# Raw inputs in four loads with tiles of their own, and the output's decays through a DRAM scratch

## The chip, the cores and the metric

The kernel runs on one core of a Trainium2 chip. The metric is the device time of one execution in microseconds (us). Three runs of the kernel before took 1276.74, 1278.87 and 1279.15 us; their median, 1278.87, is the time before.

## What is computed

A recurrent attention runs over 768 positions for 4 x 8 batches and heads, each with a 40 x 40 state. Its output becomes the 3072 x 320 input of two dense layers in a row, each with 2048 hidden units.

```python
for t in range(S):                                        # r,k,v,w,a,b: (4, 8, 768, 40)
    y[:, :, t] = np.einsum('bhd,bhde->bhe', rt, state)
    Sa = np.einsum('bhde,bhe->bhd', state, at)
    state = state * wt[:, :, None, :] - np.einsum('bhd,bhe->bhde', Sa, bt) \
            + np.einsum('bhd,bhe->bhde', vt, kt)
x = y.transpose(0, 2, 1, 3).reshape(B * S, H * D)         # (3072, 320)
h = x @ w_in;   x = (h / (1 + exp(-h))) @ w_out           # first layer
h = x @ w2_in;  out = (h - tanh(h)) @ w2_out              # second layer
```

## The kernel before

The sequence is cut into 12 chunks of 64 positions, and a chunk into two halves of 16 heads (`hf` 0 and 1). In the first phase (to about 930 us) the attention of the chunks and the first layer run interleaved; in the second phase only the second layer runs. Weights are converted from float32 pairs on the way (lines 515 to 557: DMA into `cr`, then work on ACT, DVE and POOL; the second layer's go to a DRAM scratch `w2d`).

Within a chunk, each half goes through these steps.

- `load_raw` (L196) loads everything that the half's preparation needs in one DMA of 120 partitions x 2311 floats into the tile `raw`: 384 columns of a, 768 of k and b, 384 of r, 384 of v, 391 of w. `raw` has one buffer, so the load waits until the preparation before has read its last column (the POOL subtraction of L241). For half 1 of chunk 0, a free slot of the ring `LR` serves instead.
- `prep` (L210) makes the scaled operands. DVE scans w into `pq` (L226: the running product of the decays, restarted for each head), takes a reciprocal into `d1b` (L227), writes two columns of decays to `HL` (L228, L229), multiplies a by `pq` (L231), scans w backward into the same tile `pq` (L232: the inverse decays), and multiplies k and b by them (L235). ACT and POOL split the products into a high and a low float16 part in the tile `HL`, which has one buffer. Twelve DMAs (L252) then copy `HL` into a slot of the five-slot ring `LR`, three partition blocks of 40 each. A slot of the ring comes free when PE has used a half of an earlier chunk (its last readers are `ch_y` and `ch_x`).
- p1, sol, mrg, x, u, s, y and m are the attention proper: PE matmuls with evictions on ACT and DVE. `sol_step` is a forward substitution of 31 pairs of DVE instructions (L311, L313). The lows of u and of the state are copied across partitions by SP DMAs (`LR<-LR`, `LR<-lows` at L390; `MT` at L447 and L448; `M` at L477 and L478).
- `pf_load` (L480) loads the decays once more, in the layout of the transposed output (feature by position), from an input `wf` that the host packs: 128 x 384 floats into the one-buffered tile `pf`. `pf_scan` (L485) scans them on DVE (L487). `x_t1` transposes the output y on PE, and `x_t2` multiplies it by `pf` on DVE (L504) and splits it into xh and xl (ACT L505, POOL at the helper line L191), which also frees `pf`.

The order in which the instructions are written comes from a table of times (`SC`) and from dependencies (`when`); a scheduler then sets each engine's own order, and each engine runs its list strictly in that order. All DMAs stand in one list, that of SP. Each DMA takes one of eight counters in turn, and a DMA waits for the one that used its counter before. A DMA that waits holds up all behind it.

Of the kernel before, what the change touches and what calls it, by code (L numbers as in the profile page):

```python
# [13 lines left out]
ALU = mybir.AluOpType  # L14
# [33 lines left out]
def _poly():  # L48
# [46 lines left out]
    ps=(2.4285, 5.4475),  # L95
# [10 lines left out]
def build(tc, pk, tv, wf, w1i, w1o, w2i, w2o, out, nch=NCH, dbg=None):  # L106
# [41 lines left out]
    d1f = const.tile([128, 6, C], F16, name="d1f")  # L148
    POOL.memset(d1f, 0.0)
    POOL.memset(d1f[:, :, 0:1], P_INIT * S_X / (S_R * S_M))  # L150
# [37 lines left out]
    y_t, ps_t, x_t, pf_t = {}, {}, {}, {}  # L188

# [20 lines left out]
    def prep(c, hf):  # L210
        raw = raw_t.pop((c, hf))
# [20 lines left out]
        DVE.tensor_tensor_scan(pt[:, 2:391][:, ::-1], w[:, 2:391][:, ::-1], d1b[:, 2:391][:, ::-1], 0.0, ALU.mult, ALU.add)  # L232
        pi = pt[:, 2:392].rearrange("p (j t) -> p j t", t=65)[:, :, 0:C]
# [4 lines left out]
        pscale(raw[:, 1152:1920], raw[:, 1152:1920], S_R)  # L238
# [57 lines left out]
    def lr_slot():  # L296
        return at_p.tile([128, 16, RW], F16, tag="LR", name="LR", bufs=5)
# [198 lines left out]
    def x_t2(c, hf):  # L496
# [7 lines left out]
        DVE.tensor_tensor(xf, ps, xf, ALU.mult)  # L504
# [150 lines left out]
    for c in range(nch):  # L655
# [83 lines left out]
def pack(inputs, nch=NCH):  # L739
# [7 lines left out]
    def zero_first(x):  # L747
        return np.concatenate([np.zeros_like(x[..., :1]), x], axis=-1)
# [6 lines left out]
    wv = np.asarray(inputs["w"]).reshape(B, H, NCH, C, D).transpose(2, 1, 4, 0, 3).reshape(NCH, DM, B, C)  # L755
    wv = zero_first(wv[..., :-1]).reshape(NCH, DM, B * C)
    wf = np.stack([wv[:, 0:128], wv[:, 128:256], np.concatenate([wv[:, 256:320]] * 2, axis=1)], axis=2)
    wf = wf.reshape(NCH, 128, 3, 2, 128).transpose(0, 3, 1, 2, 4)

# [5 lines left out]
    def w_out(m):  # L765
# [3 lines left out]
        "pk": pk[:nch], "tv": tv[:nch], "wf": wf[:nch],  # L769
# [20 lines left out]
```

## Time and profile before

| | |
|---|---|
| median of three runs | 1278.87 us |
| profiled execution, device time | 1283.47 us |
| its span (first to last instruction) | 1281.4 us |
| PE, DVE, ACT, POOL busy in the span | 1063.9, 971.2, 822.5, 421.6 us |
| mean granted TensorE clock, share of full speed | 0.932 |
| DMAs moved | 122.36 MB in 154955 packets |

The profile is one execution, so its times add up to 1281.4 us of span and 2.1 us around it. The share of busy time is a mean over three stages: a prologue of about 160 us, in which PE has little to do; the stage from 160 to 885 us, in which attention and first layer run together; and the rest, in which PE is nearly full. A DVE or PE instruction that is late holds up everything behind it on its engine, so a wait matters where the engine is the one that others wait for.

### The profile page before, as it was taken

To read this page: it belongs to the slowest core of one execution; us is meant where nothing else is said; L and a number is where in the kernel's file an instruction comes from. 1 tells how busy PE (TensorE), PEld (TensorE's weight loads), DVE (VectorE), ACT (ScalarE), POOL (GpSimd) and SP (SyncE) were. 2 spreads that over 40 slices of the span, in tenths; PEclk is the share of its full clock that TensorE was granted. 3 is DMA by queue.
4 is the path that set the end of the run, shared out by engine and by line. 5 is a ranking of instruction groups with operands and counts; after the bars stand their busy time and mean duration, and the time that the engine had idled before them with its cause. 6 is when DMAs were issued, how large, how long until landed. Compare 5 with 4: busy or idle time off the path is not lost.

```text
span 1281.4 us, 31698 instructions
## 1 busy us (share of the span) xinstructions
PE 1063.9 (83%) x12624; PEld 879.2 (69%) x12624; DVE 971.2 (76%) x1871; ACT 822.5 (64%) x1586; POOL 421.6 (33%) x490
## 2 busy tenths in 40 slices
PE   0006578798889889889888998999999999999997
PEld 0005566677677667767776777888778888888885
DVE  6678998788887868878677787853238788888885
ACT  2456687666767657645545454554259888888886
POOL 5334544434424333423232231010013333333332
PEclk9999759879898979989897998999989999999999
DMA  5565665555656554353424432110701111111100
GB/s 129 144 146 154 173 155 138 146 146 147 159 143 171 141 160 114 101 116 96 108 74 96 108 94 74 31 47 21 216 24 24 24 33 27 33 25 24 24 12 21
DMA packets 154955, 122.36 MB, mean 95 GB/s; under 512 B 89528, under 2 KB 140152, under 8 KB 151928
## 3 DMA queue, kind: packets, MB, share of 16 engines
q1 hardware_dynamic: 154808, 120.35, 36.5%
q8 instruction: 99, 1.62, 0.5%
q14 instruction: 48, 0.39, 0.1%
HBM read 63.59 MB, written 13.89 MB: 60 GB/s over the span
## 4 chain that ended last, share of the span: by engine, by line
PE 22%; issue 18%; DMA 17%; DVE 17%; POOL 9%; SPq 8%; ACT 8%; POOLq 0%; DVEq 0%; ACTq 0%
DMA raw<-pk 8%; POOL gl L191 7%; PE hp L567 7%; SPq L252 5%; DMA LR<-HL 3%; DVE Tl L313 3%; DVE tmp L311 2%; PE o L589 2%; PE o L591 2%; PE o L590 2%; DMA pf<-wf 2%; SPq L632 2%; PE psx L361 2%; PE psu L376 1%; ACT cr L525 1%
## 5 line engine op out<-in xcount | busy, mean ns | idle before, releaser
L567 PE MATMUL hp<-xh,wih 128*128 128x256 f16 x960 | 196.7, 291 | 13.9 <-DVE gl L577 13.7
L567 PE MATMUL hp<-x,w 128*128 128x256 f16 x1344 | 189.5, 273 | 0.0
L191 POOL TENSOR_TENSOR gl<-q,gh 128x512 f16<-128x512 f32 x96 | 111.3, 1159 | 207.8 <-ACT gh L624 207.8
L567 PEld LDWEIGHTS <-wih 128*128 128x128 f16 x1344 | 131.9, 103 | 39.5 <-issue 15.4
L567 PEld LDWEIGHTS <-w 128*128 128x128 f16 x1344 | 131.5, 98 | 22.9
L313 DVE TENSOR_TENSOR Tl<-Tl,tmp 128x126 f32<-128x126 f32 (+22 forms) x372 | 130.3, 350 | 7.6
L311 DVE TENSOR_TENSOR tmp<-Al,Tl 128x126 f32<-128x126 f32 (+22 forms) x372 | 120.4, 324 | 8.2 <-ACT Al L303 1.2
L267 PE MATMUL p1a<-LR 120*128 120x64 f16 x384 | 28.5, 207 | 116.7 <-DMA LR<-HL 69.9
L589 PE MATMUL o<-woh,gh 128*128 128x320 f16 x384 | 120.0, 313 | 5.9 <-DVE x2o L600 5.3
L591 PE MATMUL o<-woh,gl 128*128 128x320 f16 x384 | 118.6, 315 | 2.7 <-DVE gl L577 2.7
L590 PE MATMUL o<-woh,gh 128*128 128x320 f16 x384 | 119.7, 312 | 0.0
L590 PE MATMUL o<-w,gh 128*128 128x320 f16 x384 | 112.5, 299 | 0.0
L589 PE MATMUL o<-w,gh 128*128 128x320 f16 x384 | 111.3, 299 | 1.4 <-ACT gh L624 1.3
L567 PE MATMUL hp<-xl,wih 128*128 128x256 f16 x384 | 111.6, 291 | 0.1
L267 PEld LDWEIGHTS <-LR 120*128 120x128 f16 x384 | 21.6, 105 | 123.5 <-issue 108.9
L591 PE MATMUL o<-w,gl 128*128 128x320 f16 x384 | 102.5, 299 | 1.0 <-POOL gl L191 1.0
L590 PEld LDWEIGHTS <-gh 128*128 128x128 f16 x768 | 76.7, 100 | 32.6 <-issue 5.5
L591 PEld LDWEIGHTS <-gl 128*128 128x128 f16 x768 | 76.4, 100 | 31.0 <-DVE gl L577 3.4
L589 PEld LDWEIGHTS <-gh 128*128 128x128 f16 x768 | 76.6, 100 | 30.0 <-ACT gh L624 2.0
L577 DVE SCALAR_TENSOR_TENSOR gl<-hp,gh 128x512 f16<-128x512 f32 x96 | 65.5, 682 | 41.2 <-ACT gh L576 37.8
L619 DVE SCALAR_TENSOR_TENSOR s<-s,z 128x512 f32<-128x512 f32 x96 | 70.7, 737 | 32.9 <-ACT s L617 31.8
L575 ACT ACTIVATE hp<-hp 128x512 f32<-128x512 f32 x96 | 56.2, 587 | 49.0 <-PE hp L568 47.0
(147 smaller groups left out, 2952.1 us busy)
## 6 DMA issues: line engine op xcount, KB each, us to landing
raw<-pk SPq DMA_DIRECT2D x23, 1083.3 KB
LR<-HL SPq DMA_DIRECT2D x92, 150.9 KB
cr<-w1i SPq DMA_DIRECT2D x16, 384.0 KB
cr<-w2i SPq DMA_DIRECT2D x16, 384.0 KB
cr<-w1o SPq DMA_DIRECT2D x16, 320.0 KB
cr<-w2o SPq DMA_DIRECT2D x16, 320.0 KB
w2d<-w2s SPq DMA_DIRECT2D x32, 160.0 KB
w<-w2d SPq DMA_DIRECT2D x4, 1280.0 KB
```

Source lines behind the costliest of these rows:

```text
L191: POOL.tensor_tensor(out, a, b, ALU.subtract)
L252: SP.dma_start(out=dst[pl * 40:pl * 40 + 40, :, d0:d0 + w], in_=src[:, :, s0:s0 + w])
L267: PE.matmul(pa[:, p, :], kb, R[:, u, p, 0:C], start=True, stop=True)
L311: DVE.tensor_tensor(tv_, Al[:, j + 1:, j:j + 1].to_broadcast([128, n, w]), Tl[:, j:j + 1, :w].to_broadcast([128, n, w]), ALU.mult)
L313: DVE.tensor_tensor(Tl[:, j + 1:, :w], Tl[:, j + 1:, :w], tv_, ALU.add)
L567: PE.matmul(o, wi[:, f, a], x[:, k], start=n == 0, stop=False)
L575: ACT.activation(out=hp, in_=hp, func=AF.Silu, scale=1.0 / (S_X * S_WI))
L577: DVE.scalar_tensor_tensor(out=gl, in0=hp, scalar=S_G, in1=gh, op0=ALU.mult, op1=ALU.subtract)
L589: PE.matmul(o, gh[:, cs], wo[:, f, 0], start=f == 0, stop=False)
L590: PE.matmul(o, gh[:, cs], wo[:, f, 1], start=False, stop=False)
L591: PE.matmul(o, gl[:, cs], wo[:, f, 0], start=False, stop=f == NF - 1)
L619: DVE.scalar_tensor_tensor(out=s, in0=s, scalar=GAMMA, in1=z, op0=ALU.add, op1=ALU.mult)
```

## The change

Two things are changed.

First, the raw inputs come in four DMAs, each into a tile of its own: w (391 columns, two buffers), a (384, two buffers), k and b together (768, one buffer), r and v together (768, one buffer). The backward scan no longer overwrites `pq`; it writes a tile `pr`.

Second, the host no longer packs `wf`. After the copies of `HL`, `prep` writes the forward scan (`pq`) to a DRAM scratch `pd`, feature by position, in four DMAs of 40 partitions with runs of 64 floats. `pf_load` reads its tile from there in three DMAs (one of 128 partitions with two runs of 128 floats each, two of 64 partitions). `pf_scan` is gone, with its constant `d1f`; the scale that stood in the constant moves into the multiplication of `x_t2`, which becomes a scalar_tensor_tensor.

```diff
     def load_raw(c, hf):
-        if c == 0 and hf == 1:
-            t = lr_slot().rearrange("p u n -> p (u n)").bitcast(F32)[0:120, 0:RAWN]
-        else:
-            t = at_p.tile([120, RAWN], F32, tag="raw", name="raw", bufs=1)
-        SP.dma_start(out=t, in_=pk[c, hf])
-        raw_t[c, hf] = t
+        spare = lr_slot().rearrange("p u n -> p (u n)").bitcast(F32)[0:120] if c == 0 and hf == 1 else None
+        raw_t[c, hf] = []
+        for nm, o, n, k in (("w", 1920, 391, 2), ("a", 0, 384, 2), ("kb", 384, 768, 1), ("rv", 1152, 768, 1)):
+            t = spare[:, o:o + n] if spare is not None else at_p.tile([120, n], F32, tag="raw" + nm, name="raw" + nm, bufs=k)
+            SP.dma_start(out=t, in_=pk[c, hf, :, o:o + n])
+            raw_t[c, hf].append(t)
...
         pt = at_p.tile([120, 392], F32, tag="pq", name="pq", bufs=1)
+        pr = at_p.tile([120, 392], F32, tag="pr", name="pr", bufs=1)
...
-        DVE.tensor_tensor_scan(pt[:, 2:391][:, ::-1], w[:, 2:391][:, ::-1], d1b[:, 2:391][:, ::-1], 0.0, ALU.mult, ALU.add)
-        pi = pt[:, 2:392].rearrange("p (j t) -> p j t", t=65)[:, :, 0:C]
+        DVE.tensor_tensor_scan(pr[:, 2:391][:, ::-1], w[:, 2:391][:, ::-1], d1b[:, 2:391][:, ::-1], 0.0, ALU.mult, ALU.add)
+        pi = pr[:, 2:392].rearrange("p (j t) -> p j t", t=65)[:, :, 0:C]
...
+        for i, j0, n, u in ((0, 0, 6, 0), (1, 0, 2, 0), (1, 2, 4, 1), (2, 0, 4, 1)):
+            h = 6 * i + j0 - 8 * u
+            SP.dma_start(out=pd[c, hf, 40 * h:40 * (h + n), u].rearrange("(h d) t -> d h t", d=40),
+                         in_=pq[40 * i:40 * i + 40, j0:j0 + n, 0:C])
...
     def pf_load(c, hf):
         t = at_p.tile([128, 3, 128], F32, tag="pf", name="pf", bufs=1)
-        SP.dma_start(out=t, in_=wf[c, hf])
+        v = pd[c, hf].rearrange("f u t -> f (u t)")
+        SP.dma_start(out=t[:, 0:2], in_=v[0:256].rearrange("(k p) n -> p k n", k=2))
+        for q in range(2):
+            SP.dma_start(out=t[64 * q:64 * q + 64, 2], in_=v[256:320])
         pf_t[c, hf] = t
-
-    def pf_scan(c, hf):
-        t = pf_t[c, hf].rearrange("p k n -> p (k n)")
-        DVE.tensor_tensor_scan(t, t, d1f.rearrange("p b t -> p (b t)"), 0.0, ALU.mult, ALU.add)
...
-        DVE.tensor_tensor(xf, ps, xf, ALU.mult)
+        DVE.scalar_tensor_tensor(out=xf, in0=ps, scalar=S_X * S_KB / (S_R * S_M), in1=xf, op0=ALU.mult, op1=ALU.mult)
```

The scheduler's order moves with it, at three places that the prediction speaks of. Line numbers of the changed kernel differ by a few from those before.

DVE at the start, the first preparation and the beginning of the second. Before:

```order
L226 SCALAR_TENSOR_TENSOR pq<-raw,d1a 120x390
L227 RECIPROCAL d1b<-pq 120x6
L228 TENSOR_SCALAR HL<-pq 120x6
L231 SCALAR_TENSOR_TENSOR raw<-raw,pq 120x384
L229 SCALAR_TENSOR_TENSOR HL<-pq,HL 120x6
L487 SCALAR_TENSOR_TENSOR pf<-pf,d1f 128x384
L232 SCALAR_TENSOR_TENSOR pq<-raw,d1b 120x389
L235 TENSOR_TENSOR raw<-raw,pq 120x768
L226 SCALAR_TENSOR_TENSOR pq<-LR,d1a 120x390
```

After:

```order
L222 SCALAR_TENSOR_TENSOR pq<-raww,d1a 120x390
L223 RECIPROCAL d1b<-pq 120x6
L224 TENSOR_SCALAR HL<-pq 120x6
L227 SCALAR_TENSOR_TENSOR rawa<-rawa,pq 120x384
L228 SCALAR_TENSOR_TENSOR pr<-raww,d1b 120x389
L225 SCALAR_TENSOR_TENSOR HL<-pq,HL 120x6
L231 TENSOR_TENSOR rawkb<-rawkb,pr 120x768
L222 SCALAR_TENSOR_TENSOR pq<-LR,d1a 120x390
```

The scan of `pf` between the two scans of w is gone, and the backward scan (now L228) no longer stands behind the second column of `HL`.

DVE in the middle of the kernel, at the end of a chunk's substitution (`Tl`), where the second half's preparation writes `HL`. Before:

```order
L437 SCALAR_TENSOR_TENSOR Md<-psm,p_2155 40x320 [waits PE_49,Pool_49]
L323 STREAM_TRANSPOSE W_143<-Al 32x32x32 [waits Activation_49]
L324 STREAM_TRANSPOSE TT_119<-Al 64x32x32
L504 TENSOR_TENSOR pf<-psyt,pf 128x384 [waits PE_49]
L275 TENSOR_TENSOR mK_122<-p1a,mask_k 64x512 [waits PE_49]
L228 TENSOR_SCALAR HL<-pq 120x6 [waits DMAHW4_49,DMAHW7_49,DMAHW2_49,DMAHW0_49]
L437 SCALAR_TENSOR_TENSOR Md<-psm,p_2155 40x320 [waits Pool_49]
L229 SCALAR_TENSOR_TENSOR HL<-pq,HL 120x6 [waits DVE_49]
L232 SCALAR_TENSOR_TENSOR pq<-raw,d1b 120x389 [waits DVE_49]
L235 TENSOR_TENSOR raw<-raw,pq 120x768 [waits DVE_49]
```

After:

```order
L224 TENSOR_SCALAR HL<-pq 120x6 [waits DMAHW5_49,DMAHW6_49,DMAHW2_49,DMAHW0_49]
L504 SCALAR_TENSOR_TENSOR pf<-psyt,pf 128x384 [waits PE_49]
L225 SCALAR_TENSOR_TENSOR HL<-pq,HL 120x6 [waits DVE_49]
L438 SCALAR_TENSOR_TENSOR Md<-psm,p_2242 40x320 [waits Pool_49]
L276 TENSOR_TENSOR mK_119<-p1a,mask_k 64x512 [waits PE_49]
L324 STREAM_TRANSPOSE W_140<-Al 32x32x32 [waits Activation_49]
L325 STREAM_TRANSPOSE TT_116<-Al 64x32x32
L222 SCALAR_TENSOR_TENSOR pq<-raww,d1a 120x390 [waits DVE_49]
L223 RECIPROCAL d1b<-pq 120x6 [waits DVE_49]
L227 SCALAR_TENSOR_TENSOR rawa<-rawa,pq 120x384
L228 SCALAR_TENSOR_TENSOR pr<-raww,d1b 120x389 [waits DVE_49]
```

Once `HL` is free, only two short writes are left for the second half; its backward scan and its k and b product stand some 60 instructions earlier, and the rows behind are already the scans of the next chunk's first half.

SP in the middle of the kernel, from the last copies of `HL` of a half to the next raw loads. Before:

```order
L482 DMA pf<-wf 128x384
L252 DMA LR<-HL 40x4x322
L201 DMA raw<-pk 120x2311
L602 DMA x2d<-x2o 128x2x384
L557 DMA w2d<-w2s 128x640
L515 DMA cr<-w2i 128x768
L477 DMA M<-M 40x640
L478 DMA M<-lows 40x640
```

After:

```order
L199 DMA rawkb<-pk 120x768
L199 DMA rawrv<-pk 120x768
L484 DMA pf<-pd 128x2x128
L486 DMA pf<-pd 64x128 x2
L478 DMA M<-M 40x640
L479 DMA M<-lows 40x640
L256 DMA pd<-pq 40x6x64
L256 DMA pd<-pq 40x2x64
L256 DMA pd<-pq 40x4x64
L478 DMA M<-M 40x640
L479 DMA M<-lows 40x640
L256 DMA pd<-pq 40x4x64
```

Where one raw load and one load of `pf` stood, there are two raw loads (the two others stand earlier), three loads of `pf` and the four writes of `pd`, the last two of them between and behind the copies of M.

## Rows read from the trace of the kernel before

**Rows 1.** Busy time by stretch: start:end, length, PE, PEld, DVE, ACT, POOL, granted clock, DMA.

```profile
160.00:885.00 725.00, 636.38 (x8816) 529.89 (x8817) 565.75 (x1222) 442.12 (x885) 234.28 (x281) 0.90 0.44 114
400.00:480.00 80.00, 69.66 (x901) 56.74 (x901) 62.07 (x135) 49.03 (x100) 27.48 (x34) 0.85 0.59 157
320.00:400.00 80.00, 68.86 (x953) 55.99 (x951) 67.61 (x143) 60.65 (x119) 33.33 (x41) 0.91 0.56 153
800.00:880.00 80.00, 79.45 (x1215) 67.58 (x1211) 46.95 (x108) 41.01 (x84) 7.25 (x10) 0.98 0.14 36
930.00:1281.00 351.00, 342.90 (x2811) 275.42 (x2810) 272.66 (x392) 283.95 (x517) 112.59 (x99) 0.99 0.10 24
```

**Rows 2.** Chain that ended last, 160 to 885 us (first row) and pieces: start, us, what.

```profile
by line: DMA raw<-pk 13.2%; PE hp L567 7.4%; SPq L252 6.6%; issue 5.5%; DMA LR<-HL 3.7%; DVE Tl L313 3.1%; PE psx L361 2.9%; PE psu L376 2.6%; DVE tmp L311 2.4%; PE o L589 2.0%; PE o L591 1.9%; PE o L590 1.9%; PE psy L420 1.8%; PE mg L345 1
491.49 1.55 POOL HL L241
493.06 7.46 DMA raw<-pk
...
525.07 2.60 DMA LR<-HL
```

**Rows 3.** Waits, 160 to 885 us: engine, line, waited for, us, times, longest.

```profile
DVE pq L226 <- DMA raw<-pk: 40.5, 16, 4.6
DVE pf L487 <- DMA pf<-wf: 19.3, 10, 2.9
...
SPq L482 <- POOL xl L191: 23.7, 11, 6.8
...
SPq L390 <- ACT LR L386: 16.0, 6, 5.6
SPq L252 <- PE psm L429: 15.4, 5, 6.2
```

**Rows 4.** Groups of DVE instructions, 160 to 885 us: busy us, mean ns, idle before.

```profile
L487 DVE TENSOR_TENSOR_SCAN pf<-pf,d1f 128x384 f32<-128x384 f32 x22 | 22.9, 1042 | 19.4 <-DMA pf<-wf 19.3
L232 DVE TENSOR_TENSOR_SCAN pq<-raw,d1b 120x389 f32<-120x389 f32 x18 | 21.4, 1187 | 0.2
L235 DVE TENSOR_TENSOR raw<-raw,pq 120x768 f32<-120x768 f32 x18 | 20.3, 1130 | 0.2
L226 DVE TENSOR_TENSOR_SCAN pq<-raw,d1a 120x390 f32<-120x390 f32 x18 | 17.7, 981 | 40.6 <-DMA raw<-pk 40.5
```

**Rows 5.** DVE in one chunk: start, us, line, instruction, idle before it.

```profile
500.54 0.97 DVE L226 TENSOR_TENSOR_SCAN pq<-raw,d1a 120x390 f32<-120x390 f32 x1 [1.02 <-DMA raw<-pk]
...
527.79 0.18 DVE L228 TENSOR_SCALAR HL<-pq 120x6 f16<-120x6 f32 x1 [0.98 <-DMA LR<-HL]
...
534.19 0.94 DVE L235 TENSOR_TENSOR raw<-raw,pq 120x768 f32<-120x768 f32 x1
```

**Rows 6.** The prologue: start, us, engine, line, instruction, idle before it.

```profile
9.31 0.97 DVE L226 TENSOR_TENSOR_SCAN pq<-raw,d1a 120x390 f32<-120x390 f32 x1 [1.71 <-DMA raw<-pk]
...
15.65 3.81 POOL L191 TENSOR_TENSOR HL<-raw,HL 120x384 f16<-120x384 f32 x3
15.89 1.43 DVE L487 TENSOR_TENSOR_SCAN pf<-pf,d1f 128x384 f32<-128x384 f32 x1 [4.42 <-DMA pf<-wf]
17.25 1.56 DVE L232 TENSOR_TENSOR_SCAN pq<-raw,d1b 120x389 f32<-120x389 f32 x1
...
21.86 1.62 DVE L241 TENSOR_TENSOR HL<-raw,HL 120x768 f16<-120x768 f32 x1
```

**Rows 7.** DMA issues on SP: durations min/median/max in ns, and one issue of 64 partitions.

```profile
L252 SPq DMA_DIRECT2D LR<-HL x276: 767/772/1358, 12.3 to 791.1; - x138
...
L201 SPq DMA_DIRECT2D raw<-pk x23: 351/509/585, 0.8 to 750.6; - x23
...
L482 SPq DMA_DIRECT2D pf<-wf x24: 332/368/466, 1.7 to 896.6; - x24
...
515.65 0.54 SPq L207 DMA_DIRECT2D VU<-tv  x1
```

**Rows 8.** DMA packets, 160 to 885 us: queue, packets, MB, share of 16 engines.

```profile
q1 hardware_dynamic: 103966, 81.33, 43.6%
```

More of the change, by code (lines that the diff above doesn't have):

```diff
@@ L94 @@
     pl=(-0.631, 4.8433),
-    ps=(2.4285, 5.4475),
     xt=(5.6773, 6.5083),
@@ L103, with build @@
 )
-def build(tc, pk, tv, wf, w1i, w1o, w2i, w2o, out, nch=NCH, dbg=None):
+def build(tc, pk, tv, w1i, w1o, w2i, w2o, out, nch=NCH, dbg=None):
     nc = tc.nc
@@ L147, in build @@
         msk[nm] = m
-    d1f = const.tile([128, 6, C], F16, name="d1f")
-    POOL.memset(d1f, 0.0)
-    POOL.memset(d1f[:, :, 0:1], P_INIT * S_X / (S_R * S_M))
     gam = const.tile([128, 1], F32, name="gam")
@@ L188, in build @@
     y_t, ps_t, x_t, pf_t = {}, {}, {}, {}
+    pd = dram.tile([nch, 2, DM, 2, C], F32, name="pd")
     def psub(out, a, b):
@@ L210, in prep @@
     def prep(c, hf):
-        raw = raw_t.pop((c, hf))
+        w, ra, rkb, rrv = raw_t.pop((c, hf))
         hl = HL
@@ L217, in prep @@
         k0, v0 = (0, 2 * C) if c % 2 == 0 else (C, 0)
-        def sl(i, n):
-            return raw[:, i:i + 6 * n].rearrange("p (j t) -> p j t", t=n)
-        av, kb, rv, vv, w = sl(0, C), sl(384, 2 * C), sl(1152, C), sl(1536, C), raw[:, 1920:RAWN]
+        av, kb, rv, vv = [x.rearrange("p (j t) -> p j t", j=6) for x in (ra, rkb, rrv[:, 0:384], rrv[:, 384:768])]
         pt = at_p.tile([120, 392], F32, tag="pq", name="pq", bufs=1)
+        pr = at_p.tile([120, 392], F32, tag="pr", name="pr", bufs=1)
         pq = pt[:, 0:390].rearrange("p (j t) -> p j t", t=65)
@@ L237, in prep @@
         ACT.activation(out=rh[:, :, 0:C], in_=av, func=AF.Copy)
-        pscale(raw[:, 1152:1920], raw[:, 1152:1920], S_R)
+        pscale(rrv, rrv, S_R)
         ACT.activation(out=rh[:, :, C:2 * C], in_=rv, func=AF.Copy)
@@ L690, in build @@
         for hf in range(2):
-            when(T0 + SC["pl"][hf], pf_load, c, hf, after=[("x_t2", c - 1 + hf, 1 - hf)])
-            when(T0 + SC["ps"][hf], pf_scan, c, hf, after=[("pf_load", c, hf)])
+            when(T0 + SC["pl"][hf], pf_load, c, hf, after=[("prep", c, hf), ("x_t2", c - 1 + hf, 1 - hf)])
             when(T0 + SC["xt"][hf], x_t1, c, hf, after=[("ch_ye", c, 2 * hf + 1)])
-            when(T0 + SC["xt"][hf] + SC["xte"], x_t2, c, hf, after=[("x_t1", c, hf), ("pf_scan", c, hf)])
+            when(T0 + SC["xt"][hf] + SC["xte"], x_t2, c, hf, after=[("x_t1", c, hf), ("pf_load", c, hf)])
         if dbg:
@@ L754, in pack @@
     tv = np.asarray(inputs["v"]).reshape(2, 2, 8, NCH, C, D).transpose(3, 4, 0, 1, 2, 5).reshape(NCH, C, 2, 2 * DM)
[L755 to L758, printed above, removed]
     def w_in(m):
@@ L768, in pack @@
     arrays = {
-        "pk": pk[:nch], "tv": tv[:nch], "wf": wf[:nch],
+        "pk": pk[:nch], "tv": tv[:nch],
         "w1i": w_in(inputs["moe_w_in"]), "w1o": w_out(inputs["moe_w_out"]),
@@ L786 @@
     with tile.TileContext(nc, schedule_with_timeline_sim=True) as tc:
-        build(tc, aps["pk"], aps["tv"], aps["wf"], aps["w1i"], aps["w1o"], aps["w2i"], aps["w2o"], out)
+        build(tc, aps["pk"], aps["tv"], aps["w1i"], aps["w1o"], aps["w2i"], aps["w2o"], out)
     r = run_bass_kernel_spmd(nc, [arrays], core_ids=[0])
```

## The prediction

> **What bounds the kernel now.** I read the busy times by stretch first [rows 1]. From 930 us on PE is busy 342.9 of 351 us; the change touches nothing there. In the stage from 160 to 885 us PE is busy 636.4 of 725 us, so it idles 88.6 us, at a mean granted clock of 0.90; DVE is busy 565.8 us. No engine is full, and each runs its list in order, so time is lost where one engine waits for another. The chain of waits says through what [rows 2]: 13.2% of the stage, 96 us, is the raw load, from its issue to its landing, 6.6% SP issuing the twelve copies of HL, 3.7% their landing. The piece at 493 us is typical: POOL ends the last subtraction of the preparation before, the load is issued at that instant, and lands 7.46 us later. But the chain counts the whole load, and during most of it DVE has other work. What the load really costs is in the waits [rows 3]: DVE stood still 40.5 us for raw, 16 times, 4.6 us at most. It also waited 19.3 us for the load of pf, and spent 22.9 us on scanning pf, 22 times 1.04 us [rows 4].
>
> **Raw in four pieces.** The pieces w and a have two buffers, so they are loaded one preparation ahead, and the two scans and the product with a no longer wait for POOL's last subtraction. The piece with k and b (120 x 768 floats, 360 KB) still does, and so does r with v. How long such a piece takes to land no row shows. The copies of HL (40 to 151 KB) land 2.6 us after issue, the whole raw load (1083 KB) takes 7.5 us [rows 2]; in a straight line between 151 and 1083 KB, 360 KB is 2.6 + 209 x 4.9/932 = 3.7 us. Ahead of the product with k and b DVE now has both scans and more to do, 0.98 + 1.19 us alone [rows 4], so it will wait for the piece now and then. I take 36 of the 40.5 us as gone; the bounds are 0 (DVE meets the same wait at the k and b product) and 40.5.
>
> Issuing three more loads costs SP 3 x 0.51 us per half [rows 7].
>
> **HL.** A wait that the change leaves alone is that for HL. In the chunk of [rows 5] the scan ran at 500.5 us, but HL was written at 527.8 us, after a wait for the copies of the half before, and those had waited for a slot of the ring: SP stood 15.4 us for PE's psm five times [rows 3]. What changes is what follows. Before, the second scan and the k and b product stood behind the write of HL, and the half's preparation was done at 535.1 us, 7.3 us after HL came free. In the new order two short writes are left. That is work moved and not removed; it makes the copies of a second half start some 2 to 4 us earlier. I count nothing for it, since the wait for the ring slot can be the later one.
>
> **The pf path.** The scan is gone: 22.9 us of DVE in the stage [rows 4]. The multiplication of x_t2 becomes a scalar_tensor_tensor of the same size and is taken as equal. The wait for pf does not go: pf has one buffer, so the second half's load still follows POOL's subtraction of the first (SP waits for that 23.7 us, 11 times [rows 3]), and instead of the scan the multiplication waits for its landing. Three loads instead of one make it land about 1.2 us later (0.47 + 2 x 0.54 - 0.37, the 64-partition rows taken as the issue for VU [rows 7]); the scan that stood behind it took 1.04 us. The two cancel, and I put the wait at no change.
>
> **SP.** The four writes of pd cost 4 x 0.77 us, the price of a 40-partition copy [rows 7]. Per half SP gains 1.5 (raw) + 3.1 (pd) + 1.2 (pf) = 5.8 us, which is 127 us over the 22 halves in the stage. A half lasts 725/22 = 33 us, of which the twelve copies take 9.3 and the rest of the list, some fifteen issues of 0.33 to 0.81 us, about 8. So SP has room on average; what counts is what stands behind the added rows. Behind the writes of pd stand the second copies of M and the copies of u, where SP waits for ACT anyway (16.0 us for the u eviction alone [rows 3]). Only the pf loads stand inside the copies of HL, which are on the chain. I take 1.2 us for one half in each of 11 chunks, 13 us; the bounds are 0 and 127.
>
> **The Trainium skill on small transfers.** The trace: twelve copies of HL are issued 0.77 us apart, and the last lands 2.6 us after its issue [rows 2, 7], so their landings overlap. "DMA: Bandwidth & Descriptors" in the Trainium skill, section "Rules for kernel authors", advises to coalesce many small transfers into one, as under 64 KB one pays mostly overhead; its section on the anatomy of a DMA puts that at about 2.0 us plus bytes over 436 GB/s. By that the raw load would take an estimated 4.5 us whole and 10.5 us in four pieces one after the other. The measured 7.46 us for the whole differs from the page, so the measurement decides, and the rule stays as a rival below. As to the number of packets, the stage has 103966, which take 43.6% of 16 engines' time [rows 8], 0.049 us each. The change adds 640 (pd) + 256 (pf) + 360 (raw) per half, 27.6 thousand, so at the same price the share goes to some 0.55. No queue fills up by that.
>
> **The prologue.** DVE's second scan of the first half waited behind the scan of pf, which waited 4.4 us for its landing [rows 6]. Without it, the scan runs at about 10.5 instead of 17.3 us. The first copies of HL that need everything start after DVE's subtraction at 23.5 us before; now POOL's subtractions, which end at 19.5, are the later ones. That is 4 us, and the next raw load finds w and a already there. Against it stand four writes of pd. I take 5 us, with bounds 0 and 9.
>
> **The sum.** DVE is relieved of 36 + 23 = 59 us in the stage. How much reaches the end? At most all, and at least nothing; PE has 88.6 us of idle time, part of it due to DVE, part to ACT and DMAs. I take half, 30. The clock follows idle time: 0.98 granted where PE idles 0.5 of 80 us, 0.85 and 0.91 where it idles 10.3 and 11.1 [rows 1], about 0.01 per us of idle in 80. Net of SP, 17 us less idle in 725 is 1.9 in 80, or 0.019 of clock, 13 us of the 636 busy; as those stretches also hold different work, I take 7. Sum: -30 - 5 + 13 - 7 = -29 us. The profiled execution took 1283.5 us (span 1281.4 and 2.1 around it), 4.6 above the median of the runs. 1283.5 - 29 = 1254.5; against the median, 1278.9 - 29 = 1250 us. Its own range, with between a quarter and three quarters of the 59 us passed on, is 1230 to 1268.
>
> **Rivals.**
> - DVE and PE pass everything on: -59 - 5 - 10 (clock), SP in its gaps: 1205 us. For it speaks that the chain of the whole stage runs through raw; against it that ACT and the copies of HL also make PE wait. 0.13.
> - The change doesn't do for raw what it says: preparation was held by HL and the ring slot, and DVE's wait moves from the scan to the writes of HL. Then only half of the pf scans (-11) and the prologue (-5) count, against +13 for SP: 1276 us. For it speaks [rows 5]. 0.18, half of it within the bound of no change.
> - Slower: SP's list becomes the bound. Loads of k and b wait for POOL at the head of the list, and behind them stand the writes of pd, which wait for a scan, and then the copies of u for which PE's next matmuls wait. If half of the added 127 us comes on the path, it is +64 - 35 = +29: 1308 us. It decides from 35/22 = 1.6 us per half, out of 5.8. For it speaks the 6.6% of the chain that is SP already; against it that SP waits elsewhere in its list. 0.17.
> - Slower: landings add up. If four pieces land one after another, 4 x 2.6 = 10.4 instead of 7.5 us, each half's r and v come 2.9 us later, 64 us in 22 halves; half of it passed on, without raw's gain, is +32 - 11 - 5 + 13 = +29: 1308 us. The overlapping copies of HL speak against it. By the rule of the Trainium skill cited above this is what splitting does. 0.05.
>
> **How the numbers follow.** Forecast 0.47. A run of this kernel can tell about 0.2%, 2.6 us, from no change. Faster: 0.47 + 0.13 + 0.09 = 0.69; within: 0.09; slower: 0.17 + 0.05 = 0.22. For the range I leave out some 0.07 below and 0.13 above: 1212 to 1300 us.
>
> **What would show it.** Right: DVE's wait for raw in the stage falls from 40 to under 10 us, the scan of pf is gone, the multiplication of x_t2 shows some 20 us of waits for pf, PE idles about 70 us between the same points of work, at a clock of 0.91 or 0.92, and SP's list shows 0.8 us per write of pd. Wrong: a new wait of DVE or ACT for HL as large as the one for raw was; copies of u or M that PE waits for; copies of HL that are issued later after POOL's last subtraction than before.

## The result and the profile after

The changed kernel takes 1242.8 us (median of 4 runs, 1239.5 to 1247.7) against 1279.0 us (4 runs): a ratio of 0.970, 95% interval 0.967 to 0.973, 36 us faster. Its profiled execution has a span of 1245.9 us, 35.5 less than before.

The first and the last multiplication of x_t2 are nearly equal points of work in both kernels; they cut the span in three. The first row is of before, the second of after; the third is the end of the span of after, as long as the last of [rows 1]. Columns as there.

```profile
161.40:900.40 739.00, 651.78 (x9027) 543.37 (x9028) 568.81 (x1225) 447.21 (x898) 235.75 (x284) 0.90 0.44 112
```

```profile
152.80:862.20 709.40, 636.48 (x9018) 535.00 (x9016) 550.62 (x1204) 444.44 (x895) 225.59 (x283) 0.92 0.44 119
894.90:1245.90 351.00, 342.84 (x2810) 274.44 (x2808) 274.28 (x391) 282.41 (x515) 112.33 (x99) 0.99 0.10 24
```

Up to the first point the changed kernel is 8.6 us earlier (152.8 against 161.4), the stage between the points is 29.6 us shorter, and what follows is 2.7 us longer (383.7 against 381.0); its last 351 us are as before. Within the stage PE idles 72.9 us (709.4 - 636.5) instead of 87.2, and is busy 15.3 us less on as many matmuls, at a granted clock of 0.92 instead of 0.90. So half of the gain in the stage is less waiting, and half is the same products done faster. The experiments below bear out the first half; the second half they leave open.

DVE's waits in the stage after (columns as in [rows 3]):

```profile
DVE rawkb L231 <- DMA rawkb<-pk: 10.3, 9, 1.6
...
DVE pf L504 <- DMA pf<-pd: 7.3, 5, 4.0
...
DVE HL L224 <- issue: 5.8, 4, 3.0
DVE HL L224 <- DMA LR<-HL: 5.4, 6, 2.2
```

The 40.5 us ahead of the first scan are gone; 10.3 us stand ahead of the product with k and b. The groups that answer to [rows 4]:

```profile
L222 DVE TENSOR_TENSOR_SCAN pq<-raww,d1a 120x390 f32<-120x390 f32 x17 | 20.2, 1188 | 0.7 <-DMA pd<-pq 0.5
L228 DVE TENSOR_TENSOR_SCAN pr<-raww,d1b 120x389 f32<-120x389 f32 x17 | 19.8, 1167 | 0.0
L231 DVE TENSOR_TENSOR rawkb<-rawkb,pr 120x768 f32<-120x768 f32 x17 | 16.9, 991 | 10.3 <-DMA rawkb<-pk 10.3
L504 DVE SCALAR_TENSOR_TENSOR pf<-psyt,pf 128x384 f32<-128x384 f32 x23 | 12.7, 553 | 13.3 <-DMA pf<-pd 7.3 <-PE psyt L493 5.9
```

The chain that ended last, in the stage (first row) and one piece of it (start, us, what). In [rows 2] the load of raw came first with 13.2%. Here no load of a raw piece is among the heads of the list, and the piece at 524 us lasts 3.86 us where that of [rows 2] lasted 7.46. At the head stands "issue", with 13.2% instead of 5.5% in [rows 2]: time for which the profile shows nothing that was waited for.

```profile
by line: issue 13.2%; PE hp L567 7.7%; SPq L248 5.2%; DMA LR<-HL 4.4%; DMA w2d<-w2s 4.3%; DVE Tl L314 3.2%; DVE tmp L312 3.0%; PE psx L362 2.9%; PE psu L377 2.8%; ACT cr L525 2.0%; DVE pq L222 2.0%; PE mg L346 1.8%; PE o L591 1.7%; PE o L58
...
524.12 3.86 DMA rawkb<-pk
```

DVE in one chunk, to be laid beside [rows 5]. Both scans now lie ahead of the write of HL, and behind it only the product with k and b is left, which waits 1.18 us for the piece just issued:

```profile
509.70 1.10 DVE L222 TENSOR_TENSOR_SCAN pq<-raww,d1a 120x390 f32<-120x390 f32 x1
...
511.80 1.43 DVE L228 TENSOR_TENSOR_SCAN pr<-raww,d1b 120x389 f32<-120x389 f32 x1
...
523.37 0.18 DVE L224 TENSOR_SCALAR HL<-pq 120x6 f16<-120x6 f32 x1 [0.58 <-issue]
...
528.01 0.96 DVE L231 TENSOR_TENSOR rawkb<-rawkb,pr 120x768 f32<-120x768 f32 x1 [1.18 <-DMA rawkb<-pk]
```

SP's issues of the new writes and of the new loads of pf in the whole span (columns as in [rows 7]), and the stage's DMA queue:

```profile
L256 SPq DMA_DIRECT2D pd<-pq x96: 273/366/1787, 8.6 to 722.9; - x96
```

```profile
L484 SPq DMA_DIRECT2D pf<-pd x24: 365/414/499, 43.1 to 859.0; - x24
...
L486 SPq DMA_DIRECT2D pf<-pd x48: 478/522/1650, 44.4 to 860.0; - x48
```

```profile
q1 hardware_dynamic: 129152, 82.99, 43.4%
```

A write of pd is issued in 0.37 us (median), not 0.77; the three loads of pf take 1.46 us together, where the single load took 0.37. The packets of the stage rose from 104 to 129 thousand, and their share of the DMA engines stayed at what [rows 8] showed.

### The profile page after: what moved, and what is told of

It is laid out like the page before. It is cut to its first block, busy times and chain, and to the rows that moved or that the text cites. A ratio compares the mean times of both kernels' runs of the same rounds, so it can differ in the third digit from the quotient of the medians.

```text
span 1245.9 us, 32032 instructions
## 1 busy us (share of the span) xinstructions
PE 1052.8 (85%) x12624; PEld 872.8 (70%) x12624; DVE 946.9 (76%) x1847; ACT 819.3 (66%) x1586; POOL 408.7 (33%) x488
## 4 chain that ended last, share of the span: by engine, by line
issue 24%; DVE 17%; PE 17%; DMA 13%; SPq 10%; POOL 10%; ACT 8%; POOLq 0%; DVEq 0%; ACTq 0%
POOL gl L188 7%; PE hp L567 5%; SPq L248 4%; DMA LR<-HL 3%; DMA w2d<-w2s 2%; DVE Tl L314 2%; DVE tmp L312 2%; SPq L632 2%; DVE pq L222 2%; PE psx L362 2%; PE psu L377 2%; ACT cr L525 2%; DMA pd<-pq 2%; DMA rawkb<-pk 1%; DVE c L526 1%
## 5 line engine op out<-in xcount | busy, mean ns | idle before, releaser
L567 PE MATMUL hp<-xh,wih 128*128 128x256 f16 x960 | 192.9, 289 | 14.4 <-ACT xh L505 7.7
L312 DVE TENSOR_TENSOR tmp<-Al,Tl 128x126 f32<-128x126 f32 (+22 forms) x372 | 123.9, 333 | 10.9 <-ACT Al L304 3.5
L314 DVE TENSOR_TENSOR Tl<-Tl,tmp 128x126 f32<-128x126 f32 (+22 forms) x372 | 125.6, 338 | 7.4
L589 PE MATMUL o<-woh,gh 128*128 128x320 f16 x384 | 116.6, 305 | 3.3 <-DVE x2o L600 3.1
L590 PE MATMUL o<-woh,gh 128*128 128x320 f16 x384 | 116.6, 305 | 0.0
L591 PE MATMUL o<-woh,gl 128*128 128x320 f16 x384 | 114.7, 305 | 1.5 <-DVE gl L577 1.5
```

The lines of the kernel that those rows point to most:

```text
L312: DVE.tensor_tensor(tv_, Al[:, j + 1:, j:j + 1].to_broadcast([128, n, w]), Tl[:, j:j + 1, :w].to_broadcast([128, n, w]), ALU.mult)
L314: DVE.tensor_tensor(Tl[:, j + 1:, :w], Tl[:, j + 1:, :w], tv_, ALU.add)
L567: PE.matmul(o, wi[:, f, a], x[:, k], start=n == 0, stop=False)
L589: PE.matmul(o, gh[:, cs], wo[:, f, 0], start=f == 0, stop=False)
L590: PE.matmul(o, gh[:, cs], wo[:, f, 1], start=False, stop=False)
L591: PE.matmul(o, gl[:, cs], wo[:, f, 0], start=False, stop=f == NF - 1)
```

## The experiments

My theory after the result was that a half's preparation had waited for one long landing (the landing is the moment when a load's data is there), and that cutting this landing is the whole gain. The rivals: the second buffers, by which w and a are loaded a preparation ahead; tiles of their own, which free each piece earlier; the scan that DVE no longer does. The table gives every kernel by the same two points. "Raw" is what DVE waited in the stage for any load of raw inputs; the ratio is to the kernel before on the same chip.

| kernel | ratio (95%) | first x_t2 | stage | PE busy | PE idle | clock | raw |
|---|---|---|---|---|---|---|---|
| before | 1 | 161.4 | 739.0 | 651.8 | 87.2 | 0.90 | 40.5 |
| e6_noscan | 1.001 (0.999 to 1.003) | 158.8 | 740.7 | 649.8 | 91.0 | 0.91 | 54.9 |
| e2_pd_only | 0.999 (0.997 to 1.002) | 163.8 | 741.2 | 650.0 | 91.2 | 0.91 | 22.2 |
| e3_pr_only | 1.012 (1.008 to 1.015) | 164.6 | 747.3 | 659.8 | 87.5 | 0.89 | 37.0 |
| e13_two | 0.992 (0.990 to 0.995) | 158.8 | 725.9 | 637.2 | 88.7 | 0.92 | 37.3 |
| e10_one_tile | 0.972 (0.970 to 0.975) | 151.2 | 713.5 | 642.2 | 71.3 | 0.91 | 6.9 |
| e1_raw_only | 0.967 (0.964 to 0.969) | 155.5 | 700.0 | 627.3 | 72.7 | 0.92 | 1.8 |
| e1b_raw_pr | 0.978 (0.974 to 0.983) | 151.1 | 723.0 | 646.7 | 76.4 | 0.90 | 6.0 |
| e12_pf2 | 0.982 (0.978 to 0.985) | 155.4 | 719.3 | 643.4 | 75.9 | 0.91 | 3.0 |
| after | 0.970 (0.967 to 0.973) | 152.8 | 709.4 | 636.5 | 72.9 | 0.92 | 10.3 |
| e4_one_buf | 0.969 (0.965 to 0.974) | 148.5 | 707.5 | 636.3 | 71.2 | 0.92 | 7.3 |
| e5_first_pq | 0.969 (0.965 to 0.973) | 153.2 | 709.1 | 642.0 | 67.1 | 0.91 | 6.3 |
| e7_pd_twice | 0.966 (0.963 to 0.969) | 159.5 | 694.2 | 632.0 | 62.2 | 0.94 | 9.1 |
| e15_bufs | 0.980 (0.976 to 0.985) | 156.6 | 714.4 | 637.3 | 77.1 | 0.92 | 11.0 |

The column of PE's idle time falls into two groups with nothing between: 87 to 91 us where the inputs come in one load or two, 62 to 77 us where they come in four. PE's busy time does not: it is 637 to 660 us in the first group and 627 to 647 in the second. The means of the groups differ by 11.5 us, less than the kernels of one group do among themselves, so that the pieces also shorten PE's busy time isn't shown; e13_two has the idle time of before (88.7 us) and the busy time of the changed kernel (637.2 us).

### The four pieces alone (e1_raw_only)

```diff
...
-        SP.dma_start(out=t, in_=pk[c, hf])
...
+        for nm, o, n, k in (("w", 1920, 391, 2), ("a", 0, 384, 2), ("kb", 384, 768, 1), ("rv", 1152, 768, 1)):
+            t = ... at_p.tile([120, n], F32, tag="raw" + nm, name="raw" + nm, bufs=k)
+            SP.dma_start(out=t, in_=pk[c, hf, :, o:o + n])
...
```

> The kernel before with the raw load in four pieces (w and a with two buffers) and nothing else: the backward scan still overwrites pq, pf is still loaded from wf and scanned. Theory A (DVE standing still for raw is what the change mainly removed, 40.5 us of waits in the stage, half of them passed on, and a few us of clock): 18 to 26 us faster than before, 1253 to 1261. Theory B (the separate tile of the backward scan matters, because it takes the second half's preparation from behind the write of HL; the landing of the load does not): under 8 us faster. Theory C (the scan of pf, DVE work and its place in the prologue, is the larger part): under 12 us faster.

Measured: 1239.4 us against 1283.0, 43.6 us faster: more than theory A's 18 to 26, and far from the two others. DVE's waits in the stage:

```profile
DVE pf L485 <- DMA pf<-wf: 16.9, 14, 4.2
...
DVE pq L224 <- DMA raww<-pk: 1.5, 1, 1.5
...
DVE rawkb L233 <- DMA rawkb<-pk: 0.3, 1, 0.3
```

The pieces alone carry the whole gain: the wait for raw is 1.8 us, and the wait and the scan of pf, which this kernel still has, don't make it slower than the full change.

### The decays by way of DRAM, with the single load (e2_pd_only)

The changed kernel with the single raw load. Beside the decays by way of DRAM it keeps the separate tile of the reversed scan. The lines show the decays against the kernel before.

```diff
+            SP.dma_start(out=pd[c, hf, 40 * h:40 * (h + n), u]..., in_=pq[40 * i:40 * i + 40, j0:j0 + n, 0:C])
...
-        SP.dma_start(out=t, in_=wf[c, hf])
...
+        SP.dma_start(out=t[:, 0:2], in_=v[0:256].rearrange("(k p) n -> p k n", k=2))
...
-        DVE.tensor_tensor_scan(t, t, d1f.rearrange("p b t -> p (b t)"), 0.0, ALU.mult, ALU.add)
```

> The changed kernel with the raw load put back into one DMA and one tile; the separate tile for the backward scan, the writes of pd and the load of pf from there stay. Theory A: prologue -5, half of the 23 us of pf scans -11, SP +5 (a write of pd takes 0.37 us to issue): about 11 us faster than before, 1268. Theory B: 15 to 30 us faster. Theory C: 20 to 30 us faster.

Measured: 1282.0 us against 1283.0, no difference; all three theories had expected a gain.

```profile
DVE pq L224 <- DMA raw<-pk: 22.2, 8, 4.1
```

DVE is busy 540.8 us in the stage instead of 568.8, and yet PE idles 91.2 us. The 28 us of DVE time that are freed here bring nothing over the kernel before; all of DVE's waits in the stage together rose from 153.9 to 183.9 us. Its wait for raw fell by 18.3 us, and that brought nothing either, while the others rose; so the size of this wait alone doesn't tell the gain. Beside the kernel that has the separate tile and nothing else (the next one, 1297.6 us on the same chip) e2_pd_only is 15.6 us faster. Whether the way by DRAM makes good a cost of the tile, or both differences come from the order that the scheduler makes, isn't shown.

### The reversed scan in a tile of its own, alone (e3_pr_only)

```diff
+        pr = at_p.tile([120, 392], F32, tag="pr", name="pr", bufs=1)
...
-        DVE.tensor_tensor_scan(pt[:, 2:391][:, ::-1], ...
+        DVE.tensor_tensor_scan(pr[:, 2:391][:, ::-1], ...
```

> The kernel before with a tile of its own for the backward scan and nothing else. Theory A: 0 to 3 us faster, since DVE still stands still for raw. Theory B: 15 us or more faster. Theory C: no change.

Measured: 1297.6 us against 1283.0, slower by 1.2%, which none of the theories had. PE's idle time is that of before (87.5 us); PE is busy 8.0 us longer, at a lower clock, and the first x_t2 comes 3.2 us later.

```profile
DVE pq L227 <- DMA raw<-pk: 37.0, 14, 4.7
...
DVE HL L229 <- DMA LR<-HL: 14.4, 6, 3.6
```

The wait for HL grew from 5.0 to 14.4 us. Whether this comes from the tile itself or from the new order of the whole program that the scheduler makes for it, this run can't tell.

### Without the second buffers (e4_one_buf)

```diff
-        for nm, o, n, k in (("w", 1920, 391, 2), ("a", 0, 384, 2), ("kb", 384, 768, 1), ("rv", 1152, 768, 1)):
+        for nm, o, n, k in (("w", 1920, 391, 1), ("a", 0, 384, 1), ("kb", 384, 768, 1), ("rv", 1152, 768, 1)):
```

> The changed kernel with one buffer instead of two for the pieces w and a, so that each piece is loaded only once its last reader of the half before is done. Readers of w (the two scans) end early, those of a later. Theory A in its first form (loading a preparation ahead is what counts): DVE's wait moves to the scan of w and to the product with a, and 8 to 15 us of the gain are lost, 1251 to 1258. Rival (the small pieces alone do it, because each comes free as soon as its own last reader is through): within 4 us of the changed kernel.

Measured: 1241.6 us, as the changed kernel (0.969 and 0.970) and as the rival said. Loading w and a one preparation ahead is not what gains:

```profile
DVE rawkb L231 <- DMA rawkb<-pk: 4.0, 4, 1.6
...
DVE rawa L227 <- DMA rawa<-pk: 2.8, 4, 0.9
```

### Four loads into one tile (e10_one_tile)

The kernel before, with four loads into the one tile, so that no piece is freed earlier than the others.

```diff
...
+        whole = spare if spare is not None else at_p.tile([120, RAWN], F32, tag="raw", name="raw", bufs=1)
+        for nm, o, n, k in (("w", 1920, 391, 2), ("a", 0, 384, 2), ("kb", 384, 768, 1), ("rv", 1152, 768, 1)):
+            t = whole[:, o:o + n]
...
```

> The kernel before, with the four raw loads of the run e1_raw_only, but into one tile with one buffer: all four wait for the last reader of the preparation before, as the single load did, and each consumer waits for its own piece only. Theory landing (a small first piece lands 3 us after its issue instead of 7.5, which is all the scan needs): within 8 us of e1_raw_only, 1239 to 1248. Theory release (tiles of their own let w and a be loaded while POOL still subtracts k and b): DVE still waits for w after POOL's last subtraction, less than half of the gain is left, 1258 to 1275.

Measured: 1248.4 us against 1282.1, -2.8%, at the upper end of what the theory of the landing had said.

```profile
DVE pq L225 <- DMA raw<-pk: 4.3, 5, 1.5
...
DVE raw L230 <- DMA raw<-pk: 2.6, 3, 1.6
```

One half, from POOL's last subtraction of the half before on:

```profile
673.46 2.07 POOL L240 TENSOR_TENSOR HL<-raw,HL 120x768 f16<-120x768 f32 x1
675.55 1.92 SPq L203 DMA_DIRECT2D raw<-pk  x4
678.84 0.96 DVE L225 TENSOR_TENSOR_SCAN pq<-raw,d1a 120x390 f32<-120x390 f32 x1
682.62 0.83 POOL L194 TENSOR_SCALAR raw<-raw 120x768 f32<-120x768 f32 x1 [7.10 <-issue]
```

The subtraction ended at 675.53 us, SP issued the four loads from 675.55 on, and DVE's scan ran at 678.84, 3.3 us later; the single load took 7.46 us to land [rows 2]. In all the other halves of the stage, too, the first of the four loads is issued only behind that subtraction. So nothing was loaded ahead, and still the wait for raw fell from 40.5 to 6.9 us. The cut of the landing is what removes the wait. The 9 us to the kernel with tiles of their own are within what kernels with equal waits differ by (below).

### Two pieces (e13_two)

```diff
...
+        for nm, o, n, k in (("w", 1920, 391, 1), ("a", 0, 1920, 1)):
...
```

> The kernel before with two pieces instead of four, one buffer each: w, and all the rest (a, k, b, r, v) together. Only the scans' input has a tile of its own. Theory release, as far as it is about w: DVE's wait moves from the scan to the product with a, which stands right behind it, so 20 to 30 us of the gain are lost, 1260 to 1270. Theory landing: the rest lands 6 us after its issue, so also most of the gain is lost. If the scan was the only instruction that stood in the way: as fast as e1_raw_only.

Measured: 1273.0 us against 1282.1, -0.8%: as the first two theories said, and a little slower.

```profile
DVE rawa L230 <- DMA rawa<-pk: 28.8, 16, 4.0
...
DVE pq L225 <- DMA raww<-pk: 8.5, 8, 3.0
```

The scan starts earlier, and the product with a, which needs the first columns of the 900 KB rest, waits instead: 37.3 us in all, 3.2 less than before. PE's idle time is 88.7 us, so the 0.8% do not come from less waiting: PE's busy time in the stage is 14.6 us shorter than before, and why is open. For the wait, this is the bound at zero that the prediction put on the pieces, seen one instruction earlier.

### Without the scan of pf (e6_noscan)

The kernel before; the scan is left out, and x_t2 multiplies by the loaded single decays instead of their running products.

```diff
-        DVE.tensor_tensor_scan(t, t, d1f.rearrange("p b t -> p (b t)"), 0.0, ALU.mult, ALU.add)
+        pass
...
-        DVE.tensor_tensor(xf, ps, xf, ALU.mult)
+        DVE.scalar_tensor_tensor(out=xf, in0=ps, scalar=P_INIT * S_X / (S_R * S_M) / 1024, in1=xf, op0=ALU.mult, op1=ALU.mult)
```

> The kernel before with the scan of pf left out: the output is multiplied by the loaded decays of single positions, scaled down, instead of by their running products. The load of pf and its wait stay. It takes 25 us of DVE work away. Step of the prediction (half of DVE's relief passes on): 11 us in the stage and 4 to 5 in the prologue, 15 us faster, 1264 to 1268. Rival (DVE relief counts only where DVE stands in a wait that others wait for; the scan stands before a wait for pf anyway): under 5 us faster.

Measured: 1282.3 us against 1282.1, no difference, as the rival said. The stage, and DVE's waits in it:

```profile
158.80:899.50 740.70, 649.75 (x9036) 543.51 (x9037) 543.99 (x1204) 445.42 (x899) 237.15 (x284) 0.91 0.43 112
```

```profile
DVE pq L226 <- DMA raw<-pk: 54.9, 15, 6.7
```

DVE is busy 24.8 us less (568.8 to 544.0), and its waits rose by 26.1 (153.9 to 180.0), 14.4 of them for raw. With the scan gone DVE comes to the raw inputs sooner, and they land when they did.

### Each write of pd twice (e7_pd_twice)

The changed kernel, with a second write of the same data to a scratch that nobody reads: four more issues and 640 more packets per half.

```diff
+            SP.dma_start(out=pd2[c, hf, 40 * h:40 * (h + n), u].rearrange("(h d) t -> d h t", d=40),
+                         in_=pq[40 * i:40 * i + 40, j0:j0 + n, 0:C])
```

> The changed kernel with each write of pd done twice, the second time to a scratch that nobody reads: 96 more issues on SP of 0.37 us, 35 us of SP in all, and 15360 more packets of 256 bytes. Step of the prediction (13 us for all of the added issues): 3 to 8 us slower than the changed kernel. Rival (SP's list is the bound): 20 us slower or more. Rival (SP's gaps hide it): within 2 us.

Measured: 1237.8 us, a ratio of 0.966 (0.963 to 0.969) to the kernel before, not slower than the changed kernel (0.967 to 0.973).

```profile
L259 SPq DMA_DIRECT2D pd<-pq x96: 273/378/1638, 9.4 to 720.8; - x96
```

The issues added cost 0.38 us each on SP. A cost of 20 us or more is not there; one of 3 to 8 us is not seen either, but it would lie within what kernels differ by from their order alone (below).

### The first half's scan out of the way (e5_first_pq)

In the changed kernel's prologue, DVE waits for the write of pd to read pq before it scans the second half:

```profile
15.98 1.48 DVE L222 TENSOR_TENSOR_SCAN pq<-LR,d1a 120x390 f32<-120x390 f32 x1 [4.31 <-DMA pd<-pq]
```

```diff
...
+        if c == 0 and hf == 1:
+            pt = hs[:, 12 * RW:12 * RW + 784].bitcast(F32)
+        else:
+            pt = at_p.tile([120, 392], F32, tag="pq", name="pq", bufs=1)
```

> Kernel: the changed kernel, but the forward scan of half 1 of chunk 0 goes into the unused end of the ring slot that holds its HL, so that it doesn't wait until the write of pd has read the scan of half 0. In the changed kernel's prologue DVE waits 4.31 us for that read. Theory A (the prologue is a chain through this scan): the wait goes, the first multiplication of x_t2 starts 2 to 4 us earlier, and the time is 1238 to 1241 against 1242.8. Theory B (the second half is waited for elsewhere, by the transposes or by the copies of LR): the first multiplication of x_t2 stays within 1 us of 152.8 and the time within 2 us of 1242.8.

Measured: 1241.7 us, as the changed kernel; the first x_t2 at 153.2 us (152.8).

```profile
15.75 1.04 DVE L226 TENSOR_TENSOR_SCAN pq<-raww,d1a 120x390 f32<-120x390 f32 x1 [4.08 <-DMA pd<-pq]
...
19.34 0.95 DVE L226 TENSOR_TENSOR_SCAN LR<-LR,d1a 120x390 f32<-120x390 f32 x1
```

The scheduler put the next chunk's scan in the freed place. That one waits for the same read of pq, 4.08 us, and the second half's scan, now free of it, runs later than before, at 19.34 us. So the first theory got no test: the wait only changed its owner. The time agrees with the second, which this doesn't prove.

### Three kernels meant to go further (e12_pf2, e1b_raw_pr, e15_bufs)

e12_pf2 is e1_raw_only with a single buffer for a, and two for pf, loaded earlier:

```diff
-        t = at_p.tile([128, 3, 128], F32, tag="pf", name="pf", bufs=1)
+        t = at_p.tile([128, 3, 128], F32, tag="pf", name="pf", bufs=2)
...
-            when(T0 + SC["pl"][hf], pf_load, c, hf, after=[("x_t2", c - 1 + hf, 1 - hf)])
+            when(T0 + SC["pl"][hf], pf_load, c, hf, after=[("x_t2", c - 1, hf)])
```

> Kernel: the kernel before with the inputs in four pieces (two buffers for w, one for the others), and the loaded outputs' decays pf in two buffers, so that a load no longer waits for the other half's multiplication. With the four pieces alone the wait for the raw inputs was gone (1239.39 us) and DVE's longest wait in the stage was its scan of pf for the load of pf, 16.9 us in 14. Theory A (this wait only holds DVE where something else would hold it a little later, since removing 23 us of DVE scan gave nothing): the wait falls to under 6 us and the time stays within 4 us of 1239. Theory B (DVE's waits are on the path, as that for raw was): some 10 us of the 16.9 pass on, 1229.

Measured: 1257.8 us; both theories fell. The wait for pf halved (16.9 to 7.7 us), and the stage became 19.3 us longer than that of e1_raw_only: PE idles 3.2 us more and is busy 16.1 us more on as many matmuls. The same product in e1_raw_only and in e12_pf2 (mean ns behind the busy us):

```profile
L565 PE MATMUL hp<-xh,wih 128*128 128x256 f16 x848 | 169.3, 287 | 8.0 <-DVE gl L575 7.9
```

```profile
L565 PE MATMUL hp<-xh,wih 128*128 128x256 f16 x841 | 173.6, 292 | 14.5 <-DVE gl L575 13.2 <-ACT xh L503 1.2
```

e1b_raw_pr is the kernel before with the four pieces (one buffer for w, two for a) and the reversed scan in its own tile:

```diff
+        for nm, o, n, k in (("w", 1920, 391, 1), ("a", 0, 384, 2), ("kb", 384, 768, 1), ("rv", 1152, 768, 1)):
...
+        pr = at_p.tile([120, 392], F32, tag="pr", name="pr", bufs=1)
```

> Kernel: the kernel before with the inputs in four pieces and the reversed scan in a tile pr of its own (one buffer for w, two for a, as room allows); the outputs' decays as before, by a load and a scan. The separate tile alone cost 14 us beside the single load (1297.6 against 1283). Theory A (that cost comes from a shifted order of the preparation against the arrival of the raw inputs, and has no ground once these come in pieces): 1237 to 1244, as with the pieces alone. Theory B (the tile itself costs, by the order of DVE and POOL that it sets): 1249 to 1256.

Measured: 1253.7 us. The tile goes with a cost of 14 us here too, as beside the single load, and as the second theory said. But in the trace that cost is again mostly PE's busy time, 19.4 us more in the stage than in e1_raw_only at a clock of 0.90, with 3.7 us more of idle time; and the changed kernel has the same tile and is at 1242.8. That the tile is the cause isn't shown.

e15_bufs is e4_one_buf with two buffers for pq and for pf, and the earlier load of pf:

```diff
-        pt = at_p.tile([120, 392], F32, tag="pq", name="pq", bufs=1)
+        pt = at_p.tile([120, 392], F32, tag="pq", name="pq", bufs=2)
...
-        t = at_p.tile([128, 3, 128], F32, tag="pf", name="pf", bufs=1)
+        t = at_p.tile([128, 3, 128], F32, tag="pf", name="pf", bufs=2)
...
```

> Kernel: the changed kernel with one buffer for each of the four pieces, two for the forward scan pq and two for pf, whose load no longer waits for the other half's multiplication. In the changed kernel DVE waits 4.8 us for pd's read of pq, 7.3 us in the stage for pf at the multiplication of x_t2 and 10.3 us for kb. Theory A (only waits for one large landing bound the stage, and these are spread and covered): both waits go and the time stays within 4 us of 1241. Theory B (they are on the path): 12 us of waits go, 8 or more of them from the time, 1233 or less.

Measured: 1255.4 us. Both waits are gone from the stage, those for pf's landing and for the read of pq, and the kernel is 14 us slower than e4_one_buf, which is outside both theories. In the profiled executions it loses 8.1 us before the first x_t2 and 6.9 in the stage.

None of the three answers its question cleanly, for one reason: an edit makes the scheduler order the whole program anew. e1_raw_only and e12_pf2 differ in buffers and in one rule alone; DVE has 1871 instructions in both, and runs them in another order. Nine kernels whose inputs come in four pieces lie between 1237.8 and 1257.8 us, and their waits for raw (1.8 to 11.0 us) don't sort them. That is the grain of these experiments, about 20 us: the kernels without the four pieces take 1273.0 to 1297.6 us and do not overlap with them, so the gain of the pieces stands above the grain; 10 us more or less in a single kernel do not. No kernel beat the changed one by more than the intervals.

## Why the prediction was right, point by point

- **What bounds the stage** was right: the load of raw, read from the chain and from DVE's waits [rows 2, 3]. Taking that wait away by itself gave -3.3%.
- **Raw in pieces.** 36 of the 40.5 us were to go; 30.2 went, 38.7 with the pieces alone. What is left stands where the bound had put it, ahead of the product with k and b. The straight line gave 3.7 us for the landing of that piece; in the chain it takes 3.85 to 3.92 us. That loading ahead mattered was wrong as a reason: e4_one_buf has the gain without it.
- **Half passes on.** The size is near, the reason mixed. Of the pieces' 38.7 us PE's idle time gave back 14.5 (87.2 to 72.7), 0.37 of it. Of the scan's 23 us it gave back nothing, where the prediction had counted half, 11.5 us. It treated DVE's time as one sum; in e6_noscan the time freed ahead of the wait for a landing was only waited longer.
- **SP.** The +13 us was the step with the wrong size. It stood for the three loads of pf inside the copies of HL, 1.2 us in every other half. Their issue takes what was counted (1.09 us more per half), but no cost of it shows: e2_pd_only, with these loads and the writes of pd, and e6_noscan, with neither, both without the scan, have stages of 741.2 and 740.7 us and 91.2 and 91.0 us of idle time. (e2_pd_only also has the separate tile, so this holds within the grain of the experiments.) The writes of pd were priced at 0.77 us, the price of copies between partitions [rows 7], and take 0.37; this went into the upper bound of 127 us and into the rival, not into the 13.
- **The two errors cancel.** The 13 us that didn't come and the 11.5 us from the scan that didn't come leave the net nearly as it was. That the forecast of 17 us less idle time came so near to the measured 14.3 is luck in this part.
- **The clock.** Worked out as 13 us, then cut to 7 for caution; PE's busy time fell by 15.3. The cut took away too much here, but the rule behind it, that the clock follows idle time, does not hold from kernel to kernel: at nearly the same idle time (75.9 and 72.7 us) e12_pf2 and e1_raw_only are 16.1 us apart in busy time, and e13_two has the busy time of the changed kernel at the idle time of before. That this term came out nearer to its first value is no support for it. What in an order sets the clock stays open.
- **pf.** The wait did move from the scan to the multiplication of x_t2, but is 7.3 us, not 20; the scan's removal wasn't needed for any of the gain.
- **HL** was rightly counted at nothing: DVE's waits for its copies are 5.0 us before and 5.4 after. Another 5.8 us stand ahead of the same write after (0.3 before) for which the profile shows no cause.
- **The prologue** was to give 5 us and gave 8.6. PE's first p1a, the first product of the attention, starts 4.5 us earlier (22.31 instead of 26.84 us). The reason given is one of two: with only the scan of pf left out (e6_noscan) it starts at 24.35 us, with the pieces alone and that scan still there (e1_raw_only) at 23.21. Nor are POOL's subtractions the later ones at 19.5 us; in the changed kernel they end at 15.8, and DVE's at 18.9. The other 4.1 us come between there and the first x_t2.
- **The sum.** -8.6 - 29.6 + 2.7 = -35.5 us of span, against -29. With the clock's term at its first value of 13 the forecast would have been -35. Two figures of the prediction do not follow from its own rates: with three quarters and a quarter of the 59 us passed on, and the clock's term moving with them, the sum gives 1230 to 1271 us against the median, not 1230 to 1268; and the first rival counts 10 us of clock for 59 us of idle time, where the forecast counted 7 for 17. Of the signs it named, the wait for raw (10.3 us, under 10 was said), the wait for pf (7.3, some 20) and the write of pd (0.37, 0.8) came out otherwise.

The rivals. That all of DVE's relief passes on fell with the scan, of which nothing did. That HL hides it needed PE's idle time to stay at 87 us; it is 72.9. That SP's list bounds it fell with e7_pd_twice, which adds 35 us of issues and is no slower. That landings add up fell with e10_one_tile, where the same bytes in four loads, none of them ahead of time, made the wait fall by 33.6 us; POOL begins to scale r and v 7.1 us after the first of the four issues in the half shown there, and up to 10.7 us where SP issued the fourth one late; with the single load it was 7.6 us in the half of [rows 2].

The rule of the Trainium skill ("DMA: Bandwidth & Descriptors", "Rules for kernel authors") to coalesce many small transfers, which it says are mostly overhead under 64 KB, is not refuted by that: the pieces have 180 to 360 KB, and the rule speaks of the cost of a transfer, while here the consumer of w's 391 columns had been waiting for all 2311. The section of that page on the anatomy of a DMA gives one transfer 2.0 us and bytes over 436 GB/s, fitted to DMAs that GpSimd issues; these are issued by SP. It would put the 360 KB piece at an estimated 2.8 us; the chain shows 3.9.

## What to carry to other kernels

Where a load is waited for by a row of consumers, look at which part the first of them needs: cutting the load so that this part lands first removed the wait here without another buffer or an earlier issue, and the cut must also serve the second consumer, as the two pieces show. Time freed on an engine ahead of the wait that ends last came back here as a longer wait (24.8 us freed, 26.1 us more of waits). And where a scheduler orders the program anew for each edit, measure its grain with a few neutral variants before giving a cause to a difference of one per cent.

## What the runs showed of the hardware that I had not expected

- A DMA that writes 40 partitions from SBUF to DRAM is issued in 0.37 us, half of the 0.77 us of the copies between partitions [rows 7].
- A quarter more packets in the stage (104,341 to 129,152 on the queue) left the share of the DMA engines nearly as it was, 42.9% of 739.0 us before and 43.4% of 709.4 us after.
- The matmuls of the stage, some 9,000 in both, take 627 and 647 us of PE in two kernels whose idle time differs by less than 4 us (e1_raw_only, e1b_raw_pr), at mean granted clocks of 0.92 and 0.90.
